# Block attention, top-2 experts and a gated MLP: the seam between attention and the first expert in a new order, the last output tile in two halves

## The chip, the cores and the metric

One core of one Trainium2 chip runs the kernel. The metric is the device time of one execution in microseconds, the median of the runs shown. TensorE, VectorE, ScalarE and GpSimd are called PE, DVE, ACT and POOL in the rows; SP is the queue that issues most DMAs. All four compute engines take their instructions in program order, each from its own queue, so an instruction that waits holds everything queued behind it on that engine.

## The reference, cut to what matters

```python
x = attention(q, k, v)        # 4 batches, 8 heads, 576 positions, head size 64, mask by blocks of 64
x = x.reshape(2304, 512)
# experts: 8 of 512 -> 1024 -> 512, two per token
logits = x @ w_gate + log1p(exp(x @ w_noise)) * noise
top2, weights = two largest of logits, softmax over the two
y = sum over the two of weight * (relu(x @ w1[e]) @ w2[e])
# MLP: 512 -> 2048 -> 512
h = y @ w_in
out = (h * clip(h + 3, 0, 6) / 6) @ w_out
```

Every large product is computed from rounded parts: a float32 operand is split into a rounded part (a copy on ACT, names ending in h: `wah`, `xh`, `hh`) and the rest (operand minus rounded part, names ending in l: `wal`, `xl`, `hl`), and each block of a product is three matmuls: high by high, high by low, low by high (`mm3`, L457 to L459, for the first layer; L1122 to L1124 for the second). A "rest" in this text is one such subtraction.

## The kernel before, in words

The program has three stages. Attention handles 16 pairs of heads, four pairs to a batch; the experts follow in 64 steps (expert, eighth of the hidden layer) plus a few; the MLP follows on groups of four token tiles.

The order of instructions in the attention stage, and in the seam behind it, is set by a planner that runs when the kernel is built (class `Plan`). Each operation is added with its engine and an assumed duration, what it depends on, and a priority; the lower the number, the sooner. `run` walks through time: whenever an engine is free, the open operation of the lowest priority number is issued on it. If an `urgent` bound is given, operations under that bound are "hot": another operation is held back, up to four times, when a hot one is about to become ready within `part` times its own duration. An operation with two engines in its cost table may be issued on either. `port=True` keeps the planner from placing such an operation on VectorE while one is planned on GpSimd, and the reverse. The planner only fixes the order on each engine; when an instruction really starts is decided on the chip.

There are two plans, one after the other. The first (`plan`) holds the attention stage. Its end, for the last pair of heads, is: the final product `fin` (L853), which writes two PSUM banks with 64 columns of output and 16 columns of gate and noise logits per chunk; `x_out` (L859), which scales these into `x`, for the last pair split into the logit columns (128x80) and the main columns (128x320), one each per bank; `lsum` (L870), which adds the logits to `lg` on VectorE; and, beside them, two early tiles of the first expert (AHEAD = 2): gathered by GpSimd from the finished batches (`early_load`, L448), transposed (`x_tr`, L425), copied rounded on ACT (`x_hi`, L428) and subtracted on VectorE (`x_lo`, L433).

The second plan (`plan2`) is the seam. The first expert's work on the two early tiles runs on TensorE, eight first-layer blocks `s1` (12 matmuls of 128x256 each) and eight second-layer blocks `s2` (6 matmuls of 128x512 each), while the last batch is routed (`route`, about 50 small steps, mostly VectorE, beginning with `zc` at L528, with `pos` at L571 and `idm` at L616 on TensorE and the token numbers `ids` at L630 at its end). An `s1` needs the weights' rest `wal`, an `s2` the weights' rest `wbl` and the hidden layer's rest `hl` (`h_lo`, L484) behind its rounded part `hh` (L480). The weights' splits are `wops`: ACT copy at L408, rest at L412. The pair of weights of u = 0 is already split in the first plan (PRE). When the token numbers are known, GpSimd gathers the other three tiles (`load_x`, L1091), they are transposed and split (`xops`), and the regular steps begin with the first `s1` of 368 columns. The constants of both plans stand in the table PR: 'last' is the priority of the first routing step, 'wa' and 'wb' those of the splits, 'h' with 'fh' and 'fl' those of the hidden layer's two parts, 's2', 'f1' and 'f2' those of the blocks on TensorE, 'xt' that of `xops`, 'hold' is `part`, and 'wl' and 'lsel' choose the cost tables of the weights' rests and of ten steps of the route.

At the very end, `m_s2` writes four output tiles of 128x512 from PSUM, alternating DVE (L1499) and ACT (L1497), each stored by one DMA from the SP queue (L1502).

Of the kernel before, what the change touches and what calls it, by code (L numbers as in the profile page):

```python
# [7 lines left out]
F32 = mybir.dt.float32  # L8
# [6 lines left out]
OP = mybir.AluOpType  # L15
# [28 lines left out]
QSE = ({"DVE": 0.45}, {"POOL": 1.77}, {"ACT": 0.55}, {"DVE": 0.45, "ACT": 0.55})  # L44
WLS = ({"DVE": 1.2}, {"DVE": 1.14, "POOL": 2.4}, {"POOL": 2.4, "DVE": 1.14}, {"POOL": 2.4})
VHS = ({"POOL": 2.3}, {"DVE": 0.42}, {"POOL": 2.3, "DVE": 0.42}, {"DVE": 0.42, "POOL": 2.3}, {"ACT": 0.65, "DVE": 0.42})
PR = {'last': -400, 'ranks': 30, 'rows': -20.0, 'hold': 0.5, 'na': 185.6, 'nb': 352.4, 'lsel': (0, 0, 0, 0, 0, 0, 0, 1, 0, 0), 'f1': (-81.8, 24.7, 6.3, 59.0, -0.2, -63.6, -25.8, 17.6), 'f2': (-4.4, -9.0, -4.1, -76.6, 2.1, -7.1, 6.5, -47.2), 'fa': (-4.3, -4.4, -2.8, 81.4), 'fb': (10.5, -52.7, -45.1, -19.0), 'fh': (-82.6, 22.1, -3.3, -0.4, 24.6, -39.7, -3.6, -72.4), 'fl': (-15.2, 94.0, 43.5, -100.3, 0.8, -76.5, -19.7, 1.6), 'v': -315.73, 'qk': -55.37, 'keep': 1, 'S': 9.04, 'max': -280.34, 'exp': -161.48, 'pt': -15.17, 'hi': 83.56, 'hid': True, 'av': 18.28, 'o': -48.5, 'od': True, 'inv': -240.77, 'fin': 204.7, 'x': -99.74, 'route': 17.68, 'rp': 1, 'route2': -140.2, 'xt': -550.8, 'eg': 594.74, 'ex': 458.19, 'ew': 2239.12, 'first': 0, 'sel': 2, 'vh': 3, 'wl': 1, 'wa': -657.9, 'wb': -101.5, 'h': -105.8, 's2': -43.7, 'vs': (-20.6, 9.99, -35.58), 'vpt': (-0.86, 4.61, -5.4, -4.07, 10.04, 9.83, 18.45, -3.3), 'vp': (57.91, -8.69), 'vf': (23.48, -31.17), 'qe': 1, 'vmax': (-14.96, -14.1, 4.28, -1.49, -1.85, 1.55, -8.85, 4.24, 17.81), 'vexp': (8.68, -1.7, 10.68, 1.91, -0.09, 4.69, -24.46, 2.21, 0.2)}
CLAMP = 122879.9921875


# [136 lines left out]
def kernel(  # L187
# [239 lines left out]
    def x_hi(key, t, ps):  # L427
        nc.scalar.copy(xT[key][0][:, :, t * 128:(t + 1) * 128], ps)  # L428

    def x_lo(key, t, ps):  # L430
        sl = slice(t * 128, (t + 1) * 128)
        hi, lo = xT[key]
        nc.vector.tensor_tensor(lo[:, :, sl], ps, hi[:, :, sl].bitcast(F32), op=OP.subtract)  # L433
# [224 lines left out]
    with actx:  # L658
# [229 lines left out]
        for p in range(NPAIR):  # L888
# [74 lines left out]
            for h in range(2):  # L963
                if last:
                    xs.append(add(dve(NC * 2 * E), lambda e, g=gs[h], p=p, h=h: x_out(g, p, h, slice(D, FW)),
                                  [k["F", p], k["inv2", p]] + old, -2000, drop=gs[h]))
                w = D if last else FW
                k["x", p, h] = add(dve(NC * w), lambda e, g=gs[h], p=p, h=h, c=slice(0, w): x_out(g, p, h, c),
                                   [k["F", p], k["inv2", p]] + old, u0 + NU + PR["x"], drop=gs[h])
                if not last:  # L970
                    xs.append(k["x", p, h])
            k["ls", p] = add({"DVE": 0.4} if last else {"POOL": 0.7}, lambda e, p=p: lsum(e, p),
# [9 lines left out]
        for t in range(AHEAD):  # L982
            key = ("qk"[t], 0)
            k["eg", t] = add({"POOL": 1.04}, lambda e, t=t, key=key: early_load(t, raw[key]),
                             [k["r", B - 2], k["X", NPAIR - NP2 - 1]] + ([k["S", NPAIR - 2, u] for u in range(NU)] if t else [k["qs", NPAIR - 2]]), PR["eg"] + t, lat=2.4)
            g = Bank("t", PR["keep"])
            tr = add({"PE": 0.44}, lambda e, t=t, g=g: x_tr("a", xn["a", t], t, AHEAD * 128, tb[g.bank].rearrange("p (k n) -> p k n", k=KD)), [k["eg", t]], PR["ex"] + t, take=g)
            hi_ = add({"ACT": 0.48}, lambda e, t=t, g=g: x_hi("a", t, tb[g.bank].rearrange("p (k n) -> p k n", k=KD)), [tr], PR["ex"] + t, drop=g)
            k["ex", t] = add({"DVE": 0.6}, lambda e, t=t, g=g: x_lo("a", t, tb[g.bank].rearrange("p (k n) -> p k n", k=KD)), [hi_], PR["ex"] + t, drop=g)
        for n_, (w, u) in enumerate(PRE):  # L990
            hi_ = add({"ACT": 0.95}, lambda e, w=w, u=u: split_hi(w, u, early), [], PR["ew"] + n_, after=135.0)
            add({"DVE": 1.2}, lambda e, w=w, u=u: split_lo(w, u, e), [hi_], PR["ew"] + n_, port=True)
# [422 lines left out]
        xops(t, k2["g", t], PR["xt"] + t)  # L1415
    wops(0, NPF, [k2["s1", NF - 4], k2["s1", NF - 3]], PR["na"])
    wops(1, NPF, [k2["s2", NF - 4], k2["s2", NF - 3]], PR["nb"])
    plan2.run(busy, PR['last'] + 20, PR['hold'])
    gctx.close()
    wraw2[0] = ctx.enter_context(tc.tile_pool(name="wraw2", bufs=4, side="right", reuse_waits="tile"))  # L1420
# [69 lines left out]
    def m_s2(i, gi, f):  # L1490
        nt = len(GR[gi])
        s2(range(nt), hT.pop(("m", gi, f)), w_s[1, U0 + i], f, f == 0, f == NFF - 1)
        if f == NFF - 1:
            for t in range(nt):
                o = work.tile([128, DM], F32, tag="yo", name="yo", bufs=YB)
                if t % 2:
                    nc.scalar.mul(o, yps[t], 1.0 / 6.0)  # L1497
                else:
                    nc.vector.tensor_scalar(o, yps[t], 1.0 / 6.0, None, op0=OP.mult)  # L1499
                c, b = GR[gi][t]  # L1500
                if c:
                    nc.sync.dma_start(out[b * S + QC[c][0]:b * S + QC[c][0] + 128, :], o)  # L1502
                else:
                    for r in range(2):
                        nc.sync.dma_start(out[(b + r) * S:(b + r) * S + 64, :], o[r * 64:(r + 1) * 64])
# [65 lines left out]
```

## Time and profile before

| what | us |
|---|---|
| median of 3 runs (1014.65 to 1015.74) | 1014.91 |
| the profiled execution | 1013.64 |
| its span, first to last instruction | 1011.8 |
| TensorE busy in it | 997.2 |
| VectorE, ScalarE, GpSimd busy | 712.0, 558.3, 253.4 |

The rows of the profile carry a start in us from the first instruction, a duration, the engine, the source line, the operation, the tile written and the tiles read with their shapes, and in brackets the idle time of that engine just before and what ended it. Matmuls are pipelined: a matmul's duration is longer than the distance to the next start. A clock of 1.00 is TensorE's full level of 2.4 GHz, and 0.5 its low level of 1.2 GHz; a stretch's figure is the mean.

### The profile page before, as it was taken

The numbers are of one execution on the slowest core, as the hardware profiler recorded it, in microseconds if no ns is written. First come the engines' busy times: TensorE is split into PE (matmuls) and PEld (weight loads), VectorE is DVE, ScalarE is ACT, GpSimd is POOL, SyncE is SP. The second block draws the span as 40 slices with busy tenths as digits, with TensorE's granted clock in tenths as the row PEclk, the third lists the DMA queues.
The fourth block names the chain that finished last, engine by engine and source line by source line (L and its number), as shares of the span: only waits on it lengthen the run. The fifth ranks groups of instructions, "written<-read, shape, count | busy, mean of one in ns | idle before, by whom it ended". The sixth has DMA issues, their size and how long they took to land. (4 is left out here: it accounts for less than half of the span.)

```text
span 1011.8 us, 18246 instructions
## 1 busy us (share of the span) xinstructions
PE 997.2 (99%) x6813; PEld 831.7 (82%) x6813; DVE 712.0 (70%) x1396; ACT 558.3 (55%) x1063; POOL 253.4 (25%) x353
## 2 busy tenths in 40 slices
PE   8999998999999999999999999999999999999998
PEld 5667666889889999998888989888888888888886
DVE  6686886767898999887878667757546745754542
ACT  6878785344656565655555356655445445444442
POOL 3255645141020302020200026615204401500000
PEclk9999999999999999999999999999999999999999
DMA  6656542189999999788884263122112202201001
GB/s 155 162 162 158 153 107 56 28 290 326 290 320 285 316 250 303 209 267 196 239 227 150 69 216 104 25 70 48 46 42 63 63 1 74 49 3 42 1 1 42
DMA packets 162745, 141.85 MB, mean 140 GB/s; under 512 B 91541, under 2 KB 130549, under 8 KB 162653
## 3 DMA queue, kind: packets, MB, share of 16 engines
q1 hardware_dynamic: 146669, 102.73, 36.6%
q0 software_dynamic: 8640, 28.32, 9.2%
q10 hardware_dynamic: 7344, 9.60, 2.8%
q8 instruction: 54, 0.88, 0.4%
q14 instruction: 38, 0.31, 0.1%
HBM read 92.91 MB, written 36.70 MB: 128 GB/s over the span
## 5 line engine op out<-in xcount | busy, mean ns | idle before, releaser
L458 PE MATMUL h<-xl,wah 128*128 128x512 f32 (+8 forms) x832 | 272.4, 327 | 3.0 <-DVE xl L433 3.0
L457 PE MATMUL h<-xh,wah 128*128 128x512 f32 (+8 forms) x832 | 273.3, 328 | 1.0 <-DVE lg L870 1.0
L459 PE MATMUL h<-xh,wal 128*128 128x512 f32 (+8 forms) x832 | 272.4, 327 | 0.0
L1122 PE MATMUL y<-wbh,hh 128*128 128x512 f32 (+1 forms) x576 | 226.0, 392 | 0.1
L1123 PE MATMUL y<-wbl,hh 128*128 128x512 f32 (+1 forms) x576 | 225.8, 392 | 0.0
L1124 PE MATMUL y<-wbh,hl 128*128 128x512 f32 (+1 forms) x576 | 225.1, 391 | 0.0
L458 PEld LDWEIGHTS h<-xl,wah 128*128 128x128 f32 x832 | 157.3, 189 | 17.9 <-DVE xl L433 3.4
L457 PEld LDWEIGHTS h<-xh,wah 128*128 128x128 f32 x832 | 157.3, 189 | 16.3 <-ACT wah L408 1.1
L459 PEld LDWEIGHTS h<-xh,wal 128*128 128x128 f32 x832 | 157.4, 189 | 11.5
L480 ACT ACTIVATE hh<-h 128x288 fp32r<-128x288 f32 (+7 forms) x128 | 53.0, 416 | 138.9 <-PE h L459 133.1
L1124 PEld LDWEIGHTS y<-wbh,hl 128*128 128x128 f32 (+1 forms) x576 | 107.5, 187 | 24.6
L1122 PEld LDWEIGHTS y<-wbh,hh 128*128 128x128 f32 (+1 forms) x576 | 107.6, 187 | 21.5 <-issue 0.6
L1123 PEld LDWEIGHTS y<-wbl,hh 128*128 128x128 f32 (+1 forms) x576 | 107.6, 187 | 20.7
L1485 DVE SCALAR_TENSOR_TENSOR r<-r,h 128x512 f32<-128x512 f32 (+1 forms) x80 | 50.4, 630 | 98.5 <-ACT r L1484 98.3
L1484 ACT ACTIVATE r<-h,three 128x512 f32<-128x512 f32 (+1 forms) x80 | 51.6, 645 | 119.0 <-PE h L459 119.0
L412 DVE TENSOR_TENSOR wal<-wa,wah 128x1024 fp32r<-128x1024 f32 x79 | 105.1, 1330 | 12.5 <-ACT wah L408 11.4
L412 DVE TENSOR_TENSOR wbl<-wb,wbh 128x1024 fp32r<-128x1024 f32 x75 | 101.3, 1351 | 14.9 <-ACT wbh L408 11.5
L408 ACT CAST wbh<-wb 128x1024 fp32r<-128x1024 f32 x80 | 83.8, 1047 | 24.8 <-PE y L1124 12.2
L1487 ACT CAST hh<-r 128x512 fp32r<-128x512 f32 (+1 forms) x80 | 46.2, 577 | 84.9 <-DVE r L1485 81.4
L1488 DVE TENSOR_TENSOR hl<-r,hh 128x512 fp32r<-128x512 f32 (+1 forms) x80 | 56.1, 701 | 51.5 <-ACT hh L1487 51.0
L762 ACT ACTIVATE P<-sb,nm 128x288 f32<-128x288 f32 (+8 forms) x160 | 78.7, 524 | 18.7 <-DVE nm L753 18.7
L408 ACT CAST wah<-wa 128x1024 fp32r<-128x1024 f32 x80 | 83.7, 1046 | 2.7 <-DMA wb<-in_moe_w_dram 1.8
(245 smaller groups left out, 1285.2 us busy)
## 6 DMA issues: line engine op xcount, KB each, us to landing
wa<-in_moe_w_dram SPq DMA_DIRECT2D x23, 512.0 KB
wb<-in_moe_w_dram SPq DMA_DIRECT2D x23, 512.0 KB
y_tab<-yo SPq DMA_DIRECT2D x32, 256.0 KB
w<-in_moe_w_in_dram SPq DMA_DIRECT2D x16, 512.0 KB
y_tab<-zero SPq DMA_DIRECT2D x8, 1024.0 KB
w<-in_moe_w_out_dram SPq DMA_DIRECT2D x16, 512.0 KB
wa<-in_moe_w_dram ACTq DMA_DIRECT2D x9, 512.0 KB
wb<-in_moe_w_dram ACTq DMA_DIRECT2D x9, 512.0 KB
```

Of the source, the lines that this page charges most:

```text
L408: nc.scalar.copy(w_s[which, u][0], raws[PS[u]][which])
L412: (nc.gpsimd if e == "POOL" else nc.vector).tensor_tensor(lo, raws[PS[u]][which], hi.bitcast(F32), op=OP.subtract)
L457: nc.tensor.matmul(ps, lhsT=wh, rhs=xh, start=first, stop=False)
L458: nc.tensor.matmul(ps, lhsT=wh, rhs=xl, start=False, stop=False)
L459: nc.tensor.matmul(ps, lhsT=wl, rhs=xh, start=False, stop=last)
L480: nc.scalar.activation(h[0][:, c0:c1], ps[:, :c1 - c0], AF.Relu)
L762: nc.scalar.activation(P[i][p % PB2][:, a:b_], sb[t][:, o:o + b_ - a], AF.Exp, bias=nms[p, i], scale=1.0, accum_out=rs[p % 3][:, COL[i] + ...
L1122: nc.tensor.matmul(yps[t][:n], lhsT=hh[:, sl], rhs=wh[:, f % 2], start=first, stop=False)
L1123: nc.tensor.matmul(yps[t][:n], lhsT=hh[:, sl], rhs=wl[:, f % 2], start=False, stop=False)
L1124: nc.tensor.matmul(yps[t][:n], lhsT=hl[:, sl], rhs=wh[:, f % 2], start=False, stop=last)
L1484: nc.scalar.activation(r[:, :n], ps[:, :n], AF.Relu, bias=three, scale=1.0)
L1488: nc.vector.tensor_tensor(hl[:, :n], r[:, :n], hh[:, :n].bitcast(F32), op=OP.subtract)
```

## The change

Four edits. The priorities of the two early tiles' ACT copy and rest go from 458 to -2100 and -2099, ahead of the last pair's logits at -2000. The main columns of the last pair's `x` go from -51 (45 + 3 - 99.74) to 3000. In the second plan GpSimd's start is set no earlier than VectorE's, and PR has new values for the seam: among them 'wl' from 1 to 0 (the weights' rests have only VectorE left in their cost table), 'lsel' to zeros (all ten steps on VectorE), 'last' from -400 to -90, 'xt', 'wa', 'wb', 'h', 's2' and the tables for single blocks. The last output tile is written as two halves of 256 columns, the first by ACT with its DMA from ACT's queue, the second by VectorE with its DMA from SP's.

```diff
-PR = {'last': -400, 'ranks': 30, 'rows': -20.0, 'hold': 0.5, 'na': 185.6, 'nb': 352.4, 'lsel': (0, 0, 0, 0, 0, 0, 0, 1, 0, 0), 'f1': (-81.8, 24.7, 6.3, 59.0, -0.2, -63.6, -25.8, 17.6), 'f2': (-4.4, -9.0, -4.1, -76.6, 2.1, -7.1, 6.5, -47.2), 'fa': (-4.3, -4.4, -2.8, 81.4), 'fb': (10.5, -52.7, -45.1, -19.0), 'fh': (-82.6, 22.1, -3.3, -0.4, 24.6, -39.7, -3.6, -72.4), 'fl': (-15.2, 94.0, 43.5, -100.3, 0.8, -76.5, -19.7, 1.6),
...
+PR = {'last': -90, 'ranks': 30, 'rows': -100.0, 'hold': 0.7, 'na': 185.6, 'nb': 352.4, 'lsel': (0, 0, 0, 0, 0, 0, 0, 0, 0, 0), 'f1': (-7.7, -78.5, 1.9, 35.8, -11.4, 5.8, -1.3, 10.9), 'f2': (128.6, 69.2, -13.0, -140.5, -86.9, 16.5, 6.3, 32.9), 'fa': (3.5, -6.3, 3.7, -82.2), 'fb': (28.3, 56.6, -56.3, 27.7), 'fh': (148.8, 2.8, 10.7, 8.4, -20.0, 55.4, -4.1, 0.4), 'fl': (-1.0, 78.2, 116.7, -1.6, -2.5, 38.5, 40.6, 12.7),
...
-'xt': -550.8, 'wl': 1, 'wa': -657.9, 'wb': -101.5, 'h': -105.8, 's2': -43.7
+'xt': -1001.5, 'wl': 0, 'wa': -1044.5, 'wb': 50.1, 'h': -37.8, 's2': -206.9
...
-                                   [k["F", p], k["inv2", p]] + old, u0 + NU + PR["x"], drop=gs[h])
+                                   [k["F", p], k["inv2", p]] + old, 3000 if last else u0 + NU + PR["x"], drop=gs[h])
...
-            hi_ = add({"ACT": 0.48}, lambda e, t=t, g=g: x_hi(...), [tr], PR["ex"] + t, drop=g)
-            k["ex", t] = add({"DVE": 0.6}, lambda e, t=t, g=g: x_lo(...), [hi_], PR["ex"] + t, drop=g)
+            hi_ = add({"ACT": 0.48}, lambda e, t=t, g=g: x_hi(...), [tr], -2100 + t, drop=g)
+            k["ex", t] = add({"DVE": 0.6}, lambda e, t=t, g=g: x_lo(...), [hi_], -2100 + t, drop=g)
...
+    busy["POOL"] = max(busy["POOL"], busy["DVE"])
     plan2.run(busy, PR['last'] + 20, PR['hold'])
...
                 o = work.tile([128, DM], F32, tag="yo", name="yo", bufs=YB)
+                c, b = GR[gi][t]
+                if gi == len(GR) - 1 and t == nt - 1:
+                    r0 = b * S + QC[c][0]
+                    nc.scalar.mul(o[:, 0:DM // 2], yps[t][:, 0:DM // 2], 1.0 / 6.0)
+                    nc.scalar.dma_start(out[r0:r0 + 128, 0:DM // 2], o[:, 0:DM // 2])
+                    o2 = work.tile([128, DM], F32, tag="yo", name="yo", bufs=YB)[:, 0:DM // 2]
+                    nc.vector.tensor_scalar(o2, yps[t][:, DM // 2:], 1.0 / 6.0, None, op0=OP.mult)
+                    nc.sync.dma_start(out[r0:r0 + 128, DM // 2:], o2)
+                    continue
                 if t % 2:
                     nc.scalar.mul(o, yps[t], 1.0 / 6.0)
```

## Rows read from the trace of the kernel before

**Rows 1.** The page's part 1: busy time of TensorE, its weight loads, the others
```profile
PE 997.2 (99%) x6813; PEld 831.7 (82%) x6813; DVE 712.0 (70%) x1396; ACT 558.3 (55%) x1063; POOL 253.4 (25%) x353
```

**Rows 2.** Stretches at the seam: length, busy us by engine, TensorE's clock, DMA
```profile
170.00:180.00 10.00, 6.00 (x60) 5.53 (x50) 6.11 (x12) 4.01 (x7) 2.41 (x1) 0.83 0.20 46
180.00:190.00 10.00, 7.48 (x58) 7.15 (x57) 8.29 (x49) 3.26 (x7) 0.65 (x1) 0.91 0.00 1
190.00:200.00 10.00, 10.00 (x62) 8.48 (x62) 7.69 (x27) 3.14 (x5) 2.71 (x3) 0.92 0.08 25
```

**Rows 3.** Timeline of TensorE at the seam: start, us, what, [idle before <-releaser]
```profile
169.73 0.78 PE L853 MATMUL tb<-iw,oT 64*64 64x80 f32 x33
171.50 0.35 PE L457 MATMUL h<-xh,wah 128*128 128x256 f32 x1 [0.99 <-DVE lg L870]
174.87 0.58 PE L458 MATMUL h<-xl,wah 128*128 128x256 f32 x1 [3.02 <-DVE xl L433]
...
177.81 0.39 PE L459 MATMUL h<-xh,wal 128*128 128x256 f32 x1
178.03 0.29 PE L457 MATMUL h<-xh,wah 128*128 128x256 f32 x1
178.16 0.28 PE L458 MATMUL h<-xl,wah 128*128 128x256 f32 x1
...
187.34 0.18 PE L571 MATMUL rps<-ohb,before 128*128 128x40 bf16 x1 [2.48 <-DVE ohb L523]
...
202.88 1.38 PE L425 MATMUL xps<-ident,xn 128*128 128x128 f32 x8
...
205.47 0.33 PE L457 MATMUL h<-xh,wah 128*128 128x368 f32 x1
```

**Rows 4.** Timeline of VectorE at the seam
```profile
170.57 0.24 DVE L859 TENSOR_TENSOR x<-tb,rn 128x80 f32<-128x80 f32 x1 [0.73 <-PE tb L853]
170.87 0.48 DVE L859 TENSOR_TENSOR x<-tb,rn 128x320 f32<-128x320 f32 x1
...
174.14 0.68 DVE L433 TENSOR_TENSOR xl<-tb,xh 128x512 fp32r<-128x512 f32 x1
178.10 0.42 DVE L484 SCALAR_TENSOR_TENSOR hl<-h,hh 128x256 fp32r<-128x256 f32 x1 [3.29 <-ACT hh L480]
178.44 0.18 DVE L528 TENSOR_SCALAR zc<-lg 128x40 f32<-128x40 f32 x1
...
179.78 1.22 DVE L412 TENSOR_TENSOR wal<-wa,wah 128x1024 fp32r<-128x1024 f32 x1
...
195.74 0.20 DVE L630 SCALAR_TENSOR_TENSOR ids<-idacc 128x40 int32<-128x40 f32 x1
```

**Rows 5.** Line 870 alone on VectorE: ns min/median/max of its two, first and last start
```profile
L870 DVE TENSOR_TENSOR lg<-lg,x x2: 232/1256/2280, 171.3 to 171.5; 128x80 f32<-128x80 f32 x2
```

**Rows 6.** Timeline of GpSimd at the seam
```profile
171.31 2.41 POOL L412 TENSOR_TENSOR wal<-wa,wah 128x1024 fp32r<-128x1024 f32 x1 [2.90 <-ACT wah L408]
...
196.68 1.63 POOL L1091 DMA_INDIRECT xn<-x_tok,ids  x1 [7.04 <-DVE ids L630]
```

**Rows 7.** Timeline of ScalarE at the seam
```profile
169.70 0.58 ACT L428 CAST xh<-tb 128x512 fp32r<-128x512 f32 x1 [0.59 <-PE tb L425]
170.18 1.05 ACT L408 CAST wah<-wa 128x1024 fp32r<-128x1024 f32 x1
...
177.69 0.38 ACT L480 ACTIVATE hh<-h 128x256 fp32r<-128x256 f32 x1 [5.51 <-PE h L459]
```

**Rows 8.** Timelines of SP's queue and of ScalarE at the end
```profile
1006.59 2.27 SPq L1502 DMA_DIRECT2D out_dram<-yo  x4
...
1007.90 0.60 ACT L1497 ACTIVATE yo<-y 128x512 f32<-128x512 f32 x1 [0.76 <-PE y L1124]
```

**Rows 9.** Stretches at the end; the last two columns are the DMA share and GB/s
```profile
1008.50:1009.00 0.50, 0.00 (x0) 0.00 (x0) 0.00 (x0) 0.00 (x1) 0.00 (x0) 1.00 1.03 381
...
1010.00:1010.50 0.50, 0.00 (x0) 0.00 (x0) 0.00 (x0) 0.00 (x0) 0.00 (x0) 1.00 0.37 143
```

More of the change, by code (lines that the diff above doesn't have):

```diff
@@ L46 @@
 VHS = ({"POOL": 2.3}, {"DVE": 0.42}, {"POOL": 2.3, "DVE": 0.42}, {"DVE": 0.42, "POOL": 2.3}, {"ACT": 0.65, "DVE": 0.42})
-PR = {'last': -400, 'ranks': 30, 'rows': -20.0, 'hold': 0.5, 'na': 185.6, 'nb': 352.4, 'lsel': (0, 0, 0, 0, 0, 0, 0, 1, 0, 0), 'f1': (-81.8, 24.7, 6.3, 59.0, -0.2, -63.6, -25.8, 17.6), 'f2': (-4.4, -9.0, -4.1, -76.6, 2.1, -7.1, 6.5, -47.2), 'fa': (-4.3, -4.4, -2.8, 81.4), 'fb': (10.5, -52.7, -45.1, -19.0), 'fh': (-82.6, 22.1, -3.3, -0.4, 24.6, -39.7, -3.6, -72.4), 'fl': (-15.2, 94.0, 43.5, -100.3, 0.8, -76.5, -19.7, 1.6), 'v': -315.73, 'qk': -55.37, 'keep': 1, 'S': 9.04, 'max': -280.34, 'exp': -161.48, 'pt': -15.17, 'hi': 83.56, 'hid': True, 'av': 18.28, 'o': -48.5, 'od': True, 'inv': -240.77, 'fin': 204.7, 'x': -99.74, 'route': 17.68, 'rp': 1, 'route2': -140.2, 'xt': -550.8, 'eg': 594.74, 'ex': 458.19, 'ew': 2239.12, 'first': 0, 'sel': 2, 'vh': 3, 'wl': 1, 'wa': -657.9, 'wb': -101.5, 'h': -105.8, 's2': -43.7, 'vs': (-20.6, 9.99, -35.58), 'vpt': (-0.86, 4.61, -5.4, -4.07, 10.04, 9.83, 18.45, -3.3), 'vp': (57.91, -8.69), 'vf': (23.48, -31.17), 'qe': 1, 'vmax': (-14.96, -14.1, 4.28, -1.49, -1.85, 1.55, -8.85, 4.24, 17.81), 'vexp': (8.68, -1.7, 10.68, 1.91, -0.09, 4.69, -24.46, 2.21, 0.2)}
+PR = {'last': -90, 'ranks': 30, 'rows': -100.0, 'hold': 0.7, 'na': 185.6, 'nb': 352.4, 'lsel': (0, 0, 0, 0, 0, 0, 0, 0, 0, 0), 'f1': (-7.7, -78.5, 1.9, 35.8, -11.4, 5.8, -1.3, 10.9), 'f2': (128.6, 69.2, -13.0, -140.5, -86.9, 16.5, 6.3, 32.9), 'fa': (3.5, -6.3, 3.7, -82.2), 'fb': (28.3, 56.6, -56.3, 27.7), 'fh': (148.8, 2.8, 10.7, 8.4, -20.0, 55.4, -4.1, 0.4), 'fl': (-1.0, 78.2, 116.7, -1.6, -2.5, 38.5, 40.6, 12.7), 'v': -315.73, 'qk': -55.37, 'keep': 1, 'S': 9.04, 'max': -280.34, 'exp': -161.48, 'pt': -15.17, 'hi': 83.56, 'hid': True, 'av': 18.28, 'o': -48.5, 'od': True, 'inv': -240.77, 'fin': 204.7, 'x': -99.74, 'route': 17.68, 'rp': 1, 'route2': -140.2, 'xt': -1001.5, 'eg': 594.74, 'ex': 458.19, 'ew': 2239.12, 'first': 0, 'sel': 2, 'vh': 3, 'wl': 0, 'wa': -1044.5, 'wb': 50.1, 'h': -37.8, 's2': -206.9, 'vs': (-20.6, 9.99, -35.58), 'vpt': (-0.86, 4.61, -5.4, -4.07, 10.04, 9.83, 18.45, -3.3), 'vp': (57.91, -8.69), 'vf': (23.48, -31.17), 'qe': 1, 'vmax': (-14.96, -14.1, 4.28, -1.49, -1.85, 1.55, -8.85, 4.24, 17.81), 'vexp': (8.68, -1.7, 10.68, 1.91, -0.09, 4.69, -24.46, 2.21, 0.2)}
 CLAMP = 122879.9921875
@@ L987 @@
             tr = add({"PE": 0.44}, lambda e, t=t, g=g: x_tr("a", xn["a", t], t, AHEAD * 128, tb[g.bank].rearrange("p (k n) -> p k n", k=KD)), [k["eg", t]], PR["ex"] + t, take=g)
-            hi_ = add({"ACT": 0.48}, lambda e, t=t, g=g: x_hi("a", t, tb[g.bank].rearrange("p (k n) -> p k n", k=KD)), [tr], PR["ex"] + t, drop=g)
-            k["ex", t] = add({"DVE": 0.6}, lambda e, t=t, g=g: x_lo("a", t, tb[g.bank].rearrange("p (k n) -> p k n", k=KD)), [hi_], PR["ex"] + t, drop=g)
+            hi_ = add({"ACT": 0.48}, lambda e, t=t, g=g: x_hi("a", t, tb[g.bank].rearrange("p (k n) -> p k n", k=KD)), [tr], -2100 + t, drop=g)
+            k["ex", t] = add({"DVE": 0.6}, lambda e, t=t, g=g: x_lo("a", t, tb[g.bank].rearrange("p (k n) -> p k n", k=KD)), [hi_], -2100 + t, drop=g)
         for n_, (w, u) in enumerate(PRE):
@@ L1499, in m_s2 @@
                     nc.vector.tensor_scalar(o, yps[t], 1.0 / 6.0, None, op0=OP.mult)
-                c, b = GR[gi][t]
                 if c:
```

## Prediction

> **What bounds the kernel now.** I read the page's part 1 first: TensorE is busy for 997.2 us of the 1011.8 us span [rows 1], so an edit that adds or removes no matmul can win only from the 14.6 us in which TensorE is idle, and from stretches in which it runs at its low level. The stretches by time show next where both lie: 6.00 and 7.48 us busy of ten in 170 to 190, with a mean clock of 0.83, 0.91 and 0.92 in 170 to 200 [rows 2]. The low level is 0.5, so 0.83 over ten microseconds is 3.4 us at that level, and 0.91 with 0.92 another 3.4 us. This is the seam, where all but the last of the edits lie.
>
> TensorE's timeline says what it waits for there [rows 3]. Attention's last product ends at 170.51. The first expert's first matmul starts at 171.50; the second, which needs the rest `xl` of the second early tile, only at 174.87, after 3.02 us of idle time. Then the matmuls stand 0.22 us apart (177.81, 178.03), and from 178.03 on 0.13: the level changes there. A third idle time, 2.48 us, ends at 187.34 with the routing's `pos`, which waited for VectorE's `ohb`. The regular steps begin at 205.47.
>
> The other engines' timelines give the reason for the 3.02 us. ScalarE's rounded copy of that tile ended at 170.28 [rows 7], but on VectorE the rest started only at 174.14 [rows 4], behind the logits, one main part of `x`, both additions to `lg` and the other main part. The second addition took 2.28 us where the first took 0.232 [rows 5]: it ran from 171.50 to 173.78, and GpSimd's `wal` from 171.31 to 173.72 [rows 6]. VectorE's two-input addition stood until GpSimd's two-input subtraction was over. So the bound is VectorE's order, with GpSimd in its way.
>
> **The change, part by part.** *The early tile's rest ahead.* In the plan this rest is ready about 0.1 us before the last product's columns (copy 0.48 against product 0.67 plus assumed latencies), so at -2099 it goes first. On the chip: start 170.3, 0.68 to 171.0 [rows 4, 7]. Behind it two logit parts at 0.15 each (170.57 to 170.87), a main part at 0.4 to the next start, two additions at 0.23 [rows 4, 5], the second main part: done at 172.6. The first main part starts at 171.3 and ends at 171.8. It had ended at 171.35 when TensorE started 0.15 later at 171.50 [rows 3, 4], and I take that as the release of the PSUM bank, which this block overwrites. So the first matmul comes at 171.9, the second at 172.1 instead of 174.87: 2.8 us. It is idle for 1.4 us instead of 0.99 and 3.02. After 0.99 the first matmul still took 0.35 at the full level's pace, while the low level followed the 3.02, so I take the full level here: 15 matmuls (174.87 to 178.03, at 0.21) at 0.12, another 1.4 us. Two first-layer blocks then end at 174.8 instead of 179.1.
>
> *The main columns behind*, at 3000: no gain and no loss. Between the second logit part and `lsum` the plan still has a gap of 0.13 us in which only they are open, so the order logits, main, additions, main stays. What waits for them is the store of `x_tok`, three DMAs on SP's queue, with nothing queued behind them there until the first expert's output; it moves earlier.
>
> *GpSimd's start.* Nothing by itself: with the new table values only the gathers are left for GpSimd in the second plan, and they wait for `ids` anyway. What counts is 'wl' and 'lsel': the two GpSimd rests (2.41 us for the one shown [rows 6]) go to VectorE at 1.22 each [rows 4], and the 2.05 us of blocked addition disappear. Net VectorE has 0.4 us more to do in the seam, where it is busy for 6.1, 8.3 and 7.7 of ten [rows 2]. The gaps in it hide this; if they were gone, it costs 0.4 us.
>
> *The new priorities*, followed by hand through the planner's rule. On VectorE `wal` of the second pair comes first (172.6 to 173.8), then routing: `zc` at about 173.8 instead of 178.44 [rows 4], 4.6 us earlier, because it no longer stands behind an `hl` that waits for a late block. TensorE does the third first-layer block from 174.8 to 176.2. Then comes a **new stall**: the next block is of the second layer and needs `hl`, which now has a lower rank than every routing step; all three of its PSUM buffers are full until then. On VectorE the third pair's `wal` also stands ahead: its ACT copy needs both first blocks (174.8, plus 1.05 [rows 7], so 175.9), it takes 1.22 to 177.1, then come some 1.4 us of routing steps (an estimate: seven at 0.18 to 0.20 [rows 4]), then `hl` with 0.42, so 178.9. TensorE would be idle for 2.7 us. From below this is 0, if routing's gaps let `hl` through earlier (a step's input is ready 0.13 us after the one before it); from above 2.7 plus one more rest, 1.2. I take 2.7, since the planner holds a lower-ranked operation back four times.
>
> So at 178.9 TensorE has three blocks behind it and starts on the fourth; before it started on its third at 179.1. That is 0.2 + 1.4 = **1.6 us ahead**. After it, `pos` loses its 2.48 us wait, as routing is 4.6 us ahead: **2.5 us**. The second stretch at the low level (3.4 us by the clock, 1.5 us lost at 0.21 against 0.12) I leave in, moved behind the new stall: between 0 and 1.5, no gain taken. The last transposes, which wait for gathered tiles just before 205, lose some **0.4 us** of waits, as the gathers are further ahead than TensorE (estimated: the last two tiles' eight transposes take 1.38 us [rows 3], where eight at the 0.12 of a first-layer matmul are about 1.0). Sum: 4.5 us, steps from 201.0. The other chain agrees: `ids` at 195.74 [rows 4], less 4.6, is 191.1; from its end to the first regular matmul were 9.5 us, the gathers' issue from 196.68 [rows 6] and their landing among them, so not before 200.8. Behind this point TensorE is practically never idle until the end, so the gain stays.
>
> *The last tile in halves.* Now ACT takes 0.60 from 1007.90, and SP's fourth issue ends at 1008.86 [rows 8]. A half costs 0.38 on ACT and 0.42 on VectorE (the 128x256 forms [rows 4, 7]). Side by side the data is there 0.2 us earlier; one behind the other, 0.2 to 0.3 later. But the DMA engines are full at 381 GB/s in 1008.5 to 1009 and still busy after 1010 [rows 9]: the last tile's bytes queue behind three others. The issue on ACT's queue has nothing behind it. I take 0, ends -0.3 and +0.3. No row of before shows ACT and VectorE reading one bank at the same time. The Trainium skill (PSUM — Partial Sum Buffer, PSUM bank collisions raise a hardware error) says that two engines may not read the same bank and quadrant at once and that software has to keep them apart; by that, the halves stand one behind the other and the sum is 0.3 us less of a gain, without it 0.2 us more.
>
> **Sum.** The span goes from 1011.8 to 1007.3. The profiled execution took 1013.64, 1.84 more than its span, so 1009.1; the median of 1014.91 stands 1.27 above it, so the forecast is **1010.4**.
>
> **Rivals.** *The new stall doesn't come* (`hl` slips in early). Then 2.7 us more are won: 1014.91 - 7.2 = 1007.7. For it speaks that the plan has idle gaps between dependent steps; against it that routing and the weights' rests all rank above `hl`. Chance 0.18.
>
> *The addition's 2.28 us was not GpSimd's doing* and stays. TensorE still starts at 171.9, since its rest and bank come ahead of the second addition, but `wal`, routing and the stall's end come 2.05 later: gain 2.5, 1012.4. Against it: the two intervals end within 0.06 us of each other. Chance 0.05.
>
> *Given back*: second-layer blocks meet another stall like the first further on (each weights' pair brings an ACT copy that waits for TensorE and a rest that VectorE waits for), 2.7 us more plus about 0.4 of VectorE's added load; the gain is 1.4, time 1013.5, no measurable change. For it: VectorE is the second most loaded engine and its queue waits in order. Chance 0.16.
>
> *Slower*: routing swallows VectorE. If `hl` waits for the whole of routing, about 10 us of VectorE steps with two rests between, it comes near 186 instead of 178.9, and TensorE idles 7 us longer with three full buffers: 4.5 - 7.1 = 2.6 slower, 1017.5. It decides when the fourth block starts after 183.4 (178.9 + 4.5). For it: every routing step ranks above `hl`. Against: the planner holds each operation at most four times. Chance 0.07.
>
> *The edits do nothing* (the order on VectorE stays): 1014.9. The plan's readiness of the rest is only 0.1 us ahead of the logits, but the weights' rests leave GpSimd in any case. Chance 0.02.
>
> **Numbers.** The forecast keeps 0.52, a gain between 2.8 and 6.3 by the bounds above (stall 0 to 3.9, low level 0 to 1.5, tail 0.3 either way). A measurement of this kernel can tell about 0.2%, 2.0 us, from no change: faster means below 1012.9, slower above 1016.9. Faster: forecast, no stall, addition stays, 0.52 + 0.18 + 0.05 = 0.75; same: given back and nothing done, 0.16 + 0.02 = 0.18; slower 0.07. The range takes in the case without a stall, 1007.6, and reaches up to the edge of the given-back case, 1013.4; left out are about 2 in 10: the rest of that case, slower, and gains beyond 7.3.
>
> **What would show it.** Right: VectorE's second `xl` starts at 170.3 and both `lg` additions take 0.23; TensorE's second expert matmul at about 172.1, with the full clock in 172 to 176; no `L412` on GpSimd; `zc` near 174; an idle TensorE before the first second-layer block, ended by `hl`, about 2.7 us; `pos` no later than 183; `ids` near 191; the first 368-column matmul near 201. Wrong: that matmul after 203.5, more than one new idle time over 1.5 us on TensorE, or the clock low in more than 3.4 us. In the tail, TensorE's end to the span's end stays at 3.9 us within 0.3.

## The result and the profile after

Median 1005.94 us (1005.33 to 1007.92, four executions) against 1015.33 (1014.65 to 1016.09) for the kernel before in the same session: ratio 0.9909, 95% interval 0.9893 to 0.9924. The forecast of 1010.4 is 4.5 us too high, and the result lies below its range. The profiled execution took 1006.27, its span 1004.5, 7.3 us less than before. The rows below account for these 7.3; the medians are some 2 us further apart, since the profiled execution of the kernel before (1013.64) lies 1.7 us below the median of 1015.33, and that of the changed kernel 0.3 above its own.

Part 1 of the page after has the first surprise against [rows 1]:

```profile
PE 992.0 (99%) x6813; PEld 832.5 (83%) x6813; DVE 712.7 (71%) x1400; ACT 558.8 (56%) x1063; POOL 248.5 (25%) x350
```

As many matmuls as before are busy for 5.2 us less. An order that only takes idle time away leaves busy time as it is; here the matmuls themselves became shorter. The stretches at the seam, against [rows 2], don't show where: two of the four have the low clock for part of their time, 3.4 us each, as much as before.

```profile
170.00:180.00 10.00, 8.67 (x81) 8.35 (x74) 7.55 (x28) 5.31 (x10) 0.00 (x0) 0.83 0.16 36
180.00:190.00 10.00, 10.00 (x78) 9.06 (x77) 9.65 (x47) 4.17 (x9) 0.00 (x0) 1.00 0.00 1
190.00:200.00 10.00, 7.63 (x41) 6.05 (x41) 6.55 (x10) 3.71 (x6) 3.90 (x3) 1.00 0.42 130
200.00:210.00 10.00, 9.03 (x41) 8.18 (x42) 6.91 (x19) 4.40 (x6) 3.73 (x4) 0.83 0.42 118
```

TensorE's timeline at the seam, against [rows 3]:

```profile
169.69 0.78 PE L853 MATMUL tb<-iw,oT 64*64 64x80 f32 x33
171.81 0.55 PE L457 MATMUL h<-xh,wah 128*128 128x256 f32 x1 [1.33 <-DVE lg L870]
172.16 0.41 PE L458 MATMUL h<-xl,wah 128*128 128x256 f32 x1
...
175.15 0.29 PE L457 MATMUL h<-xh,wah 128*128 128x256 f32 x1
175.28 0.29 PE L458 MATMUL h<-xl,wah 128*128 128x256 f32 x1
...
179.03 0.40 PE L1122 MATMUL y<-wbh,hh 128*128 128x512 f32 x1
...
183.23 0.19 PE L571 MATMUL rps<-ohb,before 128*128 128x40 bf16 x1
...
200.01 0.63 PE L425 MATMUL xps<-ident,xn 128*128 128x128 f32 x4 [2.38 <-DMA xn<-x_tok,ids]
201.31 0.44 PE L457 MATMUL h<-xh,wah 128*128 128x368 f32 x1 [0.67 <-ACT xh L428]
202.04 0.44 PE L458 MATMUL h<-xl,wah 128*128 128x368 f32 x1 [0.29 <-DVE xl L433]
...
202.49 0.51 PE L457 MATMUL h<-xh,wah 128*128 128x368 f32 x1
202.79 0.51 PE L458 MATMUL h<-xl,wah 128*128 128x368 f32 x1
...
206.04 0.33 PE L457 MATMUL h<-xh,wah 128*128 128x368 f32 x1
206.21 0.34 PE L458 MATMUL h<-xl,wah 128*128 128x368 f32 x1
```

The 3.02 us wait for `xl` and the 2.48 us wait for `ohb` are gone, and no new stall stands ahead of the first second-layer block at 179.03. But the low level is there twice: 171.81 to 175.15 (matmuls 0.21 apart, then 0.13) and from 202.49 to about 205.9 (0.31 apart, then 0.17). A gather kept TensorE waiting for 2.38 us, the split of its tile for 0.67 and 0.29 more. VectorE's timeline, against [rows 4]:

```profile
170.28 0.69 DVE L433 TENSOR_TENSOR xl<-tb,xh 128x512 fp32r<-128x512 f32 x1 [0.36 <-ACT xh L428]
170.89 0.78 DVE L859 TENSOR_TENSOR x<-tb,rn 128x80 f32<-128x80 f32 x3
171.58 0.51 DVE L870 TENSOR_TENSOR lg<-lg,x 128x80 f32<-128x80 f32 x2
...
173.54 0.18 DVE L528 TENSOR_SCALAR zc<-lg 128x40 f32<-128x40 f32 x1
173.64 0.18 DVE L530 TENSOR_SCALAR zx<-lg 128x40 f32<-128x40 f32 x1
175.22 0.42 DVE L484 SCALAR_TENSOR_TENSOR hl<-h,hh 128x256 fp32r<-128x256 f32 x1 [1.40 <-ACT hh L480]
176.16 1.22 DVE L412 TENSOR_TENSOR wal<-wa,wah 128x1024 fp32r<-128x1024 f32 x1 [0.51 <-ACT wah L408]
177.30 0.19 DVE L523 TENSOR_TENSOR zx<-zx,noise 128x40 f32<-128x40 f32 x1
...
189.88 0.20 DVE L630 SCALAR_TENSOR_TENSOR ids<-idacc 128x40 int32<-128x40 f32 x1
```

The rest starts at 170.28 instead of 174.14, both additions fit into 0.51 us, `zc` comes at 173.54, and `hl` at 175.22. The 1.40 us of idle time ahead of it is its own wait for `hh`. The next routing step, `zx` times the noise, had its input at 173.82, but it stands behind `hl` and `wal` in the queue and starts only at 177.30. So the planner had put `hl` ahead of a step of higher rank.

Where the rest of the gain lies is seen at two landmarks of TensorE's timeline: the first 512-column matmul of the MLP and the kernel's last matmul. Before:

```profile
651.27 0.40 PE L457 MATMUL h<-xh,wah 128*128 128x512 f32 x1
...
1007.48 0.39 PE L1124 MATMUL y<-wbh,hl 128*128 128x512 f32 x1
```

After:

```profile
649.44 0.39 PE L457 MATMUL h<-xh,wah 128*128 128x512 f32 x1
...
1000.09 0.39 PE L1124 MATMUL y<-wbh,hl 128*128 128x512 f32 x1
```

The changed kernel is 205.47 - 201.31 = 4.16 us ahead at the first 368-column matmul, 1.83 at the MLP, and 7.39 at the end. So 2.3 us are lost behind the seam and **5.6 us are won in the MLP, which no edit touches**. The groups by line and shape, 700 to 990 us, show its matmuls. Before:

```profile
L459 PE MATMUL h<-xh,wal 128*128 128x512 f32 x210 | 83.0, 395 | 0.0
L457 PE MATMUL h<-xh,wah 128*128 128x512 f32 x210 | 82.8, 394 | 0.0
L458 PE MATMUL h<-xl,wah 128*128 128x512 f32 x210 | 82.7, 394 | 0.0
L1122 PE MATMUL y<-wbh,hh 128*128 128x512 f32 x211 | 82.3, 390 | 0.0
```

After:

```profile
L1122 PE MATMUL y<-wbh,hh 128*128 128x512 f32 x214 | 83.2, 389 | 0.0
...
L457 PE MATMUL h<-xh,wah 128*128 128x512 f32 x213 | 82.9, 389 | 0.0
L458 PE MATMUL h<-xl,wah 128*128 128x512 f32 x213 | 82.9, 389 | 0.0
L459 PE MATMUL h<-xh,wal 128*128 128x512 f32 x213 | 82.9, 389 | 0.0
```

A first-layer matmul takes 5 ns less. From start to start, the twelve of a block take 2.79 us before (902.79 to 905.58) and 2.72 after (896.96 to 899.68); the four groups of 512 columns have 64 such blocks, 4.5 us. The second layer (228 ns per start before, 226.6 after, 768 matmuls) gives about 1.

The built programs say what differs: addresses. A tile of the pool `work` gets its place when it is first asked for, and in the new order `xops` asks for `xh` and `xl` ahead of some small tiles of the routing and the scratch `r`. `xh` moves from byte 124736 of each partition to 119232, `xl` from 145216 to 139712; the weights' `wah` (55744) and `wal` (63936) stay. 124736 - 55744 = 68992 is 128 more than a multiple of 256; 119232 - 55744 = 63488 is a multiple of 256. Nothing in the change aims at this. Built with the old 'xt', the changed kernel keeps the new addresses; built with the old 'f1', 'fb', 'wl', 'wb' or 'h', one at a time, `xh` lies 128 bytes off again (these five were built, not timed).

### The profile page after: what moved, and what is told of

Same layout as the page of the kernel before. It is cut to its first block, busy times and chain, and to the rows that moved or that the text cites. A ratio compares the mean times of both kernels' runs of the same rounds, so it can differ in the third digit from the quotient of the medians.

```text
span 1004.5 us, 18248 instructions
## 1 busy us (share of the span) xinstructions
PE 992.0 (99%) x6813; PEld 832.5 (83%) x6813; DVE 712.7 (71%) x1400; ACT 558.8 (56%) x1063; POOL 248.5 (25%) x350
```

## The experiments

**Addresses without the order, the order without the addresses.** The first takes the kernel before and asks early for `xh`, `xl` and the output tile `yo`; the order of the instructions stays.

```diff
+    def touch():
+        xT[0] = work_tile([128, KD, CAP], "xh"), work_tile([128, KD, CAP], "xl")
+        pre_yo.append(work.tile([128, DM], F32, tag="yo", name="yo", bufs=YB))
...
         Q = [128, E, E]
+        touch()
```

> The kernel before, in its own order on every engine, with one thing changed: the buffers xh, xl and yo of the work pool are reserved ahead of the route's small tiles and r, so that they get the addresses they have in the changed kernel (xh at 119232 and 129472 instead of 124736 and 134976 bytes). Theory (where a matmul's moving operand lies in SBUF sets its pace): between 700 and 990 us the 128x512 matmuls of the first layer take 389 ns instead of 394 to 395, the time falls by 4.5 to 5.5 us to about 1010, and the seam stays as before, with the first 368-column matmul near 205.5. Rival (the pace comes with the new order, or differs by chip and run): no change within 1 us of the kernel before, 394 to 395 ns.

Measured: 1010.08, ratio 0.9951 (0.9935 to 0.9968), all three lines at 389 ns, the seam as before (a 3.01 us wait for `xl`, 2.48 for `ohb`). The second is the changed kernel that asks early for the routing's tiles and `r`, so that `xh` and `xl` lie where they lay before.

```diff
+        pre["key"] = work.tile([128, 16], F32, tag="off", name="key", bufs=1)[:, 0:E]
+        pre["gt"] = work.tile([128, E, E], F32, tag="rt", name="gt", bufs=1)
+        pre["idf"] = work.tile([128, E, NT], F32, tag="le", name="idf", bufs=1)
+        pre["idt"] = work.tile([128, 512], F32, tag="r", name="idt")
```

> The changed kernel with the addresses of the kernel before: the route's small tiles and r are reserved ahead of xh, xl and yo. Theory (addresses set the pace): 394 to 395 ns for the MLP's first-layer matmuls, time 4.5 to 5.5 us above the changed kernel, about 1011, so that what is left against the kernel before is the seam's share, 2 to 4.5 us. Rival (order, chip or run): 389 ns, about 1006.

Measured: 1009.65, ratio 0.9951 (0.9934 to 0.9967), 394 to 395 ns. Each half is worth 0.49%; their product, 0.9902, lies inside the changed kernel's interval. About half of the gain is the order, half the addresses. Chip and execution are ruled out as the cause of the pace: from its first to its last matmul the MLP takes 350.65 us in all eleven profiles, on at least five chips, in which the distances are multiples of 256, and 356.2 in all five in which `xh` and `xl` are 128 bytes off, the kernel before among them.

**Which distance.** In the changed kernel, bytes are reserved ahead of `xh` (64, 128, 256), or ahead of all of these tiles, weights included (128). The order stays.

```diff
+        if not pads:
+            pads.append(work.tile([128, 32], F32, tag="pad", name="pad", bufs=1))
```

> The changed kernel with 128 bytes reserved ahead of xh, xl, yo and r, so that xh lies at 119360 (the rounded weights stay at 55744). If the address itself matters below 256 bytes (64 over a multiple of 256 in the kernel before, 192 in the changed one), the first-layer matmuls of the MLP slow to 394 to 395 ns and the time rises by about 5 us. If only a coarser place matters, or none, 389 ns.

> The changed kernel with 128 bytes reserved ahead of the whole work pool, so that the weights, the hidden layer and xh all move by 128 bytes. If the place of the moving operand against the weights is what counts, the pace stays at 389 ns for both layers; if the address itself does, both layers' matmuls slow (the second layer's moving operand, wbh, moves too), by 5 us each.

> The changed kernel with 64 bytes reserved ahead of xh, xl, yo and r: the moving operand then lies 64 bytes off a multiple of 256 against the weights (128 off was slow, 0 fast). If any offset that is no multiple of 256 is slow, 394 to 395 ns in the MLP's first layer; if only 128, or a multiple of 128, is special, another figure.

> The changed kernel with 256 bytes reserved ahead of xh, xl, yo and r. If places are compared modulo 256 bytes, the pace stays at 389 ns; if modulo 512 or more, 394 to 395 ns or more.

> The changed kernel with 256 bytes per partition reserved ahead of the tiles of the moving operand, so that these tiles lie 256 bytes further; the order of the instructions is the same. If only the distance modulo 256 bytes counts: the same as the changed kernel, 1005 to 1006.5, with 389 ns per matmul in the MLP; the single look at it, 1003.6, would be an execution with the full clock in the seam. If the distance itself counts: 1003 to 1004.5 in the median as well.

One execution each took 1007.97 (128 bytes), 1006.27 (all by 128), 1007.35 (64), 1003.57 (256). Over four executions, 256 bytes gave 1004.11, ratio 0.9889 (0.9873 to 0.9906), not told apart from the changed kernel. Then one tile at a time was put 128 bytes off, the rest by a multiple of 256:

```diff
+        if nm == "xl" and not pads:
+            pads.append(work.tile([128, 32], F32, tag="pad0", name="pad0", bufs=1))
+            a = work.tile(shape, F32R, tag=nm, name=nm)
+            pads.append(work.tile([128, 32], F32, tag="pad1", name="pad1", bufs=1))
+            return a
```

> The changed kernel with the rest xl of the moving operand alone 128 bytes off; every other tile keeps its address modulo 256. If a matmul's own two operands have to agree, and also if the moving operand has to agree with the weights loaded meanwhile: the MLP's line 458 slower (its start to the next start 232 ns), lines 457 and 459 at 227, span 1.6 us (288 matmuls by 5.5 ns) longer than with no shift. If the tiles of the other engines matter: all three at 227.

> The changed kernel with the weights' rest wal alone 128 bytes off. If a matmul's own two operands have to agree: line 459 (xh by wal) slower, 232 ns or more, the others at 227. If the moving operand has to agree with the weights loaded meanwhile for the next matmul: line 458 slower (wal is loaded while xl moves), line 459 at 227. If the tiles of the other engines matter: all three at 227.

> The changed kernel with the rounded weights wah alone 128 bytes off. Own operands: lines 457 and 458 slower, line 459 at 227. Weights loaded meanwhile: lines 457 and 459 slower (wah is loaded while these move, for the next matmul), line 458 at 227. Tiles of the other engines: all three at 227.

> The changed kernel with all tiles that lie behind the moving operand 128 bytes off (the output tiles yo, the scratch r of ScalarE and VectorE, the small tables); both operands of every matmul of the MLP keep their addresses. If TensorE's own operands decide: all lines at 227 ns, span as the changed kernel's. If TensorE competes with the other engines' tiles: lines 457 to 459 at 232 to 235 as in the kernel before.

One execution each took 1005.23 (`xl`), 1010.56 (`wal`), 1009.59 (`wah`) and 1004.89 (all behind `xl`); they differ by waits and clock at the seam, too, so the pace is read from the MLP alone. The groups by line of the run with `wal` off (its lines 464, 465, 466 are 457, 458, 459 of the others, 1129 is 1122):

```profile
L465 PE MATMUL h<-xl,wah 128*128 128x512 f32 x211 | 83.6, 396 | 0.0
L466 PE MATMUL h<-xh,wal 128*128 128x512 f32 x210 | 83.4, 397 | 0.0
L1129 PE MATMUL y<-wbh,hh 128*128 128x512 f32 x212 | 82.5, 389 | 0.0
...
L464 PE MATMUL h<-xh,wah 128*128 128x512 f32 x211 | 82.1, 389 | 0.0
```

Mean ns from a matmul's start to the next one's, worked out from the starts in the whole MLP, under the line numbers of the kernel before (the next matmul is of the first layer, too, for 457 to 459, and of the second for the others), and the MLP's length in us from its first matmul's start to its last one's:

```
                     457    458    459   1122   1123   1124     MLP
before             232.5  232.1  234.7  228.1  228.2  228.0  356.21
after              227.0  226.6  226.4  227.2  226.7  226.5  350.65
order only (e2)    232.5  232.2  234.7  228.1  228.2  228.2  356.24
128 ahead of xh    232.5  232.1  234.7  228.0  228.2  228.0  356.21
64 ahead of xh     232.9  228.1  229.9  233.9  227.5  232.0  356.56
256 ahead of xh    226.7  226.9  226.4  226.9  227.0  226.4  350.65
all by 128         226.4  227.0  226.6  226.6  227.1  226.6  350.65
xl off             226.7  234.2  225.8  226.9  227.1  227.0  352.36
wal off            226.7  232.5  234.1  226.8  226.7  226.7  354.07
wah off            234.6  234.4  233.6  226.7  226.8  226.7  356.62
all behind xl off  226.4  226.7  226.9  226.5  226.9  226.9  350.65
```

The row "all by 128" says that the distance counts and not the address. The last row rules out the tiles behind `xl`, which the other engines use: with both operands in place nothing is slow. `xl` off slows the line that moves `xl` and no other. Neither of the two accounts in the expectations fits the next rows alone: with `wal` off, 459 is slow, whose own weights are off, and 458 too, behind which `wal` comes next; with `wah` off 459 is slow as well, though its own two operands agree. The first-layer columns follow this: a matmul is slow if its moving tile is not a multiple of 256 bytes from its own weights or from those of the next matmul. The last second-layer matmul ahead of a first-layer block, which the table leaves out, agrees: the next weights are `wah`, and it takes 232.5 ns with `wah` off and 226.4 to 226.9 in the other rows. The rule is fitted to these rows, most of them one execution each; no later run tested it, and three things stay open. With 64 bytes ahead of `xh`, 458 and 459 take only 228 and 230, while second-layer lines take 232 and 234 though none of their tiles had moved. The second layer takes 228 where `xh` and `xl` are 128 off. And with `wah` off, 459 ahead of a second-layer matmul takes 230.8, though both of its distances fit.

The Trainium skill (SBUF — State Buffer, Who interferes with whom) gives TensorE two read ports, one for the moving operand and one for loading weights, and calls them independent. The runs don't bear out that the two have nothing to do with each other: a shift of either tile alone by 128 bytes cost 6 to 8 ns a matmul, a shift of both together nothing. Whether the ports are where they meet, no run shows.

**Which edits make the seam.** Edits 1 and 2 alone, with the addresses of before (diff as in the change), and then with those of after:

> The kernel before with the first two edits alone: the early tiles' copy and rest at -2100, the last x at 3000. Addresses, weights' rests on GpSimd and all table values stay. Theory: the second xl starts near 170.3 and the expert's matmuls run on from 171.9 without the 3.02 us wait, but the second lg addition still takes 2.2 to 2.4 us, since GpSimd's wal still runs beside it; the first 368-column matmul comes 1 to 4 us sooner than in the kernel before, the time falls as much. Rival (the long addition held TensorE, not the order): TensorE still waits about 3 us and the time stays.

> The kernel before with the two edits of priorities (rests of the early tiles ahead, main columns of x behind) and with the addresses that the changed kernel has; the old table, the old cost tables for the weights' rests, the last tile in one piece. If the two gains add (3.3 us for the two edits, 5.0 us for the addresses, as the runs with one of them alone gave): about 1006.2, first-layer matmuls of the MLP at 389 ns, first 368-column matmul near 203.2 as with the old addresses. Then the whole new table is worth what is left to the changed kernel, 0 to 1.5 us. If the gain of the two edits holds with the old addresses only (a matter of the tiles in the seam): 1009 to 1010.

1011.19, ratio 0.9962 (0.9948 to 0.9976), and 1005.07, ratio 0.9901 (0.9883 to 0.9919). With the first, the 3.02 us wait is gone though an addition is still long: the first of the two ends 0.10 us after GpSimd's `wal`. VectorE's and GpSimd's timelines in it:

```profile
170.82 0.69 DVE L433 TENSOR_TENSOR xl<-tb,xh 128x512 fp32r<-128x512 f32 x1 [0.62 <-ACT xh L428]
...
172.12 2.46 DVE L870 TENSOR_TENSOR lg<-lg,x 128x80 f32<-128x80 f32 x2
...
171.81 2.40 POOL L412 TENSOR_TENSOR wal<-wa,wah 128x1024 fp32r<-128x1024 f32 x1 [3.60 <-ACT wah L408]
```

GpSimd alone taken out of the weights' rests and the route, in the kernel before:

```diff
-'lsel': (0, 0, 0, 0, 0, 0, 0, 1, 0, 0), ... 'wl': 1
+'lsel': (0, 0, 0, 0, 0, 0, 0, 0, 0, 0), ... 'wl': 0
```

> The kernel before with 'wl' 0 and 'lsel' zeros alone: the weights' rests and the ten steps have only VectorE left, all priorities and the order of the early tiles' rests stay (the planner orders the seam anew around it). Addresses of xh and xl stay. Theory: without GpSimd's subtraction beside it the second lg addition takes 0.23 us like the first, xl starts about 2 us sooner. Rival (the length is the addition's own): still about 2.3 us. The time moves by less than 4 us either way, VectorE having 2.4 us more to do and 2.05 less to wait.

1013.84, ratio 0.999 (0.998 to 0.9999). Both additions took 0.50 us together, so their length was GpSimd's doing, and the wait for `xl` fell to 0.97; but a `wal` came late on VectorE later on (TensorE waited 1.68 us, until 192.75), and nearly all was given back. Last, the changed kernel with edits 1 and 2 undone:

```diff
-... [tr], -2100 + t, drop=g)
+... [tr], PR["ex"] + t, drop=g)
...
-... 3000 if last else u0 + NU + PR["x"], drop=gs[h])
+... u0 + NU + PR["x"], drop=gs[h])
```

> The changed kernel with the two edits of priorities undone, the new table kept, and the addresses of the changed kernel. If the long wait for the second early tile's rest is the only large loss of the seam: an idle time of about 1 us ahead of the second matmul of the first expert instead of 3.0 (the additions are short without GpSimd's subtraction), the first 368-column matmul 1 to 2.5 us later than in the changed kernel, 1006.5 to 1008.5. If the table brings the whole gain by itself: 1005.9, as the changed kernel. If the table without the edits is worth nothing, as the part of it that leaves GpSimd out was alone: 1010.

1006.61, ratio 0.9929 (0.9907 to 0.9951). At the changed kernel's addresses: neither part 0.9951, the table with the halves 0.9929, the two priorities 0.9901, all 0.9909 (and 0.9885 in a second session). So the two priorities give the whole of the seam's gain that can be told apart from noise, and what the new table adds to them lies within the intervals. In the profiles it wins the 2.48 us wait for `ohb`, which the kernel with the two priorities still has, but TensorE waits 3.34 us at the regular steps, for the last gather and its split, where that kernel waits 0.29. The low level came twice in both.

**The clock behind the gaps.** Ten matmuls whose products nobody reads (an addition to the work, six ahead of the second plan and four behind it) keep TensorE busy in the two gaps.

```diff
...
+    fill(f"y{NT - 1}", 6)
     plan2.run(busy, PR['last'] + 20, PR['hold'])
+    fill("h", 4)
```

> The changed kernel with ten matmuls added whose products nobody reads: six of 128x512 in bfloat16 behind attention's last product, where TensorE waits for the first expert, and four ahead of the regular steps, where it waits for the gathered tiles. If the low level of the clock behind these two gaps comes from TensorE's idleness in them: full clock in 170 to 180 and in 200 to 210, 1004.0 to 1005.5 (up to 3 us of low level less, minus what the added matmuls push back). If the level does not depend on the gaps: 1006 to 1007.5, the added matmuls costing up to 1 us. If the changed kernel had the full clock there anyway on this chip: no difference from pad256_timed.

> The changed kernel unchanged, on the chip of the next run. If the low level behind the gaps costs what its matmuls' pace says (0.41 instead of 0.28 us each over some 3 us): its executions spread by 1 to 4 us, the longer ones with the lower mean clock (0.996 to 0.998 against 1.0), median 1 to 2.5 us above that of the kernel with filled gaps. If the difference came with the chip: no difference from it, and no relation between clock and time.

> The changed kernel with ten matmuls that nobody reads in the two gaps, six ahead of the first expert and four ahead of the regular steps. If the low level comes from the gaps: clock 0.999 to 1.0 in nearly every execution and 1003 to 1004, with less spread than the changed kernel. If not: the same median as the changed kernel's, or up to 1 us above it for the added matmuls.

The first run of it: 1003.34, ratio 0.9885 (0.9868 to 0.9901). Its stretches have the full clock in both places, with TensorE busy throughout the first:

```profile
170.00:180.00 10.00, 10.00 (x105) 8.57 (x104) 8.39 (x30) 6.29 (x12) 0.00 (x0) 1.00 0.26 58
...
200.00:210.00 10.00, 9.89 (x52) 8.73 (x52) 8.76 (x23) 3.32 (x5) 5.71 (x5) 1.00 0.74 242
```

In a second session, on one chip, the changed kernel took 1003.92 (1002.66 to 1006.1; ratio 0.9885, 0.9864 to 0.9905), the filled one 1002.94 (1002.24 to 1003.91; 0.9879, 0.9862 to 0.9895). Their medians are 1 us apart, within the intervals, so it isn't shown to be faster. Clock and span go together, though: the changed kernel's spans are 1000.8 and 1000.9 at a mean clock of 1.0, 1003.0 to 1004.5 at 0.997 and 0.998, and 1006.1 at 0.994; the filled kernel's eight are 1000.4 to 1003.4 at 0.999 and 1.0. The clock isn't all of it: the 1003.4 has the full clock throughout the seam and the experts, but TensorE waits there 1.22 us for a rest at 599.3 and 0.76 for a gather at 211.2, and the 1000.4 has no wait over 0.2 there.

## Why the prediction failed, point by point

*The early tile's rest ahead*: right. `xl` at 170.28 (170.3), first matmul at 171.81 (171.9), second at 172.16 (172.1).

*Full level there*: wrong in this execution. It was taken from one row, where 0.99 us of idle time was followed by the full level; here 1.33 us was followed by the low one, 1.4 us lost. Of twelve profiled executions with this order and 1.33 us of waiting six began low (first matmul 0.54 or 0.55 us) and six full (0.36). One row of a level that goes either way was no price; the ends were 0 and 1.4.

*GpSimd*: right in cause; the rival that the addition's 2.28 us was not GpSimd's falls. The bank's release by the first main part is borne out, too: with the two priorities alone the first matmul started at 172.35, while the addition that the brackets name ran on.

*New stall, 2.7 us*: wrong, the rival "the new stall doesn't come" is what happened. The failed step is "`hl`, which now has a lower rank than every routing step" as a reason that it comes last. The planner gives a free engine to what is open, whatever its rank, and by its assumed times the next routing step opened 0.13 us after `zx`. Four times it had held `hl` back, all four just before `zx` (seen in the planner's own times, printed while the kernel is built); with these used up, `hl` went into that gap. The prediction counted the four and named the 0.13 us only as a bound.

*`pos` and routing*: right. No wait for `ohb` at 183.23; `ids` at 189.88 (191).

*Transposes lose waits, second low stretch stays*: the stretch stayed, at 202.49 to 205.9. The waits grew: 2.38 us for a gather.

*Sum at the first regular matmul*: 4.16 us against 4.5, right by errors that offset: 2.7 more from the stall that didn't come and 1.5 more because the second low stretch lay behind this point, less 1.4 at the first low level and 3.05 for the gather and its copy (2.38 and 0.67). That this landmark fits is luck.

*"Behind this point TensorE is practically never idle until the end, so the gain stays"*: **the step that failed**. Idle time is one of two ways in which TensorE's time can change; the length of its matmuls is the other, and it was taken as fixed because no matmul was edited. In this execution 4.16 fell to 1.83: 0.5 us went at the first three regular matmuls, where `xl` was late, 1.6 at the low level from 202.49 to 205.9, 0.2 later. Then 5.56 came from the pace in the MLP. 1.83 + 5.56 = 7.39 is the span's 7.3 within rounding. The new table, priced as an order of issue alone, also set addresses. With the addresses of before, the changed order took 1009.65 in the median, inside the range and 0.8 from the forecast: what was forecast is about what the order gives, by the luck of the offsets above, and the term that was missing is the addresses.

*From the span to the median*: of the 4.5 us by which the forecast was off, 2.8 lie in the span (1007.3 against 1004.5). The other 1.7 lie in the way from the span to the median, taken over from the kernel before as 3.1 us and measured as 1.4.

*The bounds*: those named for stall, low level and tail make a gain of 3.0 to 9.0 us when they are added up, not 2.8 to 6.3.

*The signs*: of those of being wrong, the clock's came (low for 6.8 us, where 3.4 was the limit); the first regular matmul was not late, and only one new idle time was over 1.5 us. Of those of being right, the full clock and the stall did not come, and `pos` came at 183.2, not by 183; the others did.

*The tail*: 0, as taken. The timelines of ScalarE and VectorE, against [rows 8]:

```profile
1000.52 0.38 ACT L1500 ACTIVATE yo<-y 128x256 f32<-128x256 f32 x1 [0.76 <-PE y L1124]
...
1000.94 0.42 DVE L1503 TENSOR_SCALAR yo<-y 128x256 f32<-128x256 f32 x1 [0.40 <-ACT yo L1500]
```

VectorE's half waits 0.40 us for ScalarE's; from the last matmul's end to the span's end it is 4.0 us in both kernels. By the Trainium skill (PSUM — Partial Sum Buffer, PSUM bank collisions raise a hardware error) software has to keep two engines from reading the same bank and quadrant at once; the trace agrees, the halves stand one behind the other.

*The edits at nothing* (x's main columns at 3000, GpSimd's start): the built program without each has the same instructions in the same order.

## What to carry to other kernels

Compare the mean duration of the busiest engine's largest groups in both traces before explaining a difference by waits: 5 ns on a matmul that no edit touched was as much as the whole seam. Reordering where tiles are first asked for can move their addresses, so time an order with addresses held fixed, and try the addresses alone. Where the clock's level goes either way, a single profiled execution carries 1 to 3 us of it; read several executions' clocks beside their spans. A landmark that fits the forecast can do so by errors that offset, so check each term of the sum.

## What the runs showed of the hardware

A 128x512 matmul of these types takes 226 to 227 ns from start to start, or up to 235, by the distance of its tiles modulo 256 bytes; shifts of 64 and 128 bytes were slow, 256 was not. In the experts' first layer no such difference was seen: matmuls of 288 columns take 132.6 ns before and 132.5 after, those of 384 columns 175.5 and 175.7.

An addition of two 128x80 tiles on VectorE took 0.23 to 0.24 us alone and 2.19 to 2.28 beside a subtraction of 2.4 us on GpSimd, and ended 0.10 us after it.

The wait for the last gather was 0.35 to 0.57 us in nine of the twelve profiles with this order, but 2.38 in the changed kernel's first, 1.44 in its second and 1.93 in the one with `wal` off. In the first, all but four of the gather's large packets had landed by 197.54; a packet of an instruction queue, 16 KB, ran from 196.73 to 198.32, and the four came one behind another from 198.30 to 199.43. The other two show the same: the packet to 196.49 and 198.63, the last four packets from 196.48 to 197.58 and from 198.61 to 199.72. In the nine with a short wait that packet ran only after the gather had landed. So the long waits come with an instruction packet during the gather; that both run on one of the DMA engines is inferred, since the records don't name the engine.
